# Loads in one order of need, attention outputs transposed by DMA, and matmul groups in halves, in a fused attention and gated-FFN kernel

## The chip, the cores and the metric

The kernel runs on one core of one Trainium2 chip. The metric is the device time of one execution in microseconds (us). "PE" is TensorE, "PEld" its weight loads, "DVE" VectorE, "ACT" ScalarE, "POOL" GpSimd, "SP" the sequencer that issues most DMAs. The time of a run is about 2 us more than the "span" of its profile, which goes from the first to the last instruction. "Clock" is the share of TensorE's full clock that was granted, as the profile recorded it. Up to the first record of a run (13.77 us in before) the views show 1.00, which says nothing: the matmuls there ran at half clock, as the distances between their starts show. "Segment" is one of the four stretches of 512 tokens.

## The reference

An attention with a compressive memory (4 segments of 512 tokens, 32 heads of 16) and a gated FFN read the same x; a gate per token mixes the two.

```python
x = A_x                                                  # 1 x 2048 x 512, bf16
g = sigmoid((x * gate_w).sum(-1, keepdims=True))
# attention, per segment s of 512 tokens:
logits = einsum('bhqd,bhkd->bhqk', qs, ks) * scale + mask    # causal inside the segment
a_dot  = einsum('bhqk,bhkd->bhqd', softmax(logits), vs)
a_mem  = (phi(qs) @ M) / (phi(qs) @ z + 1e-6)            # memory of the earlier segments
o      = gh * a_mem + (1 - gh) * a_dot                   # gh = sigmoid(beta), per head
M, z   = M + phi(ks)^T vs, z + sum phi(ks)
a = concat(o) @ wo
# FFN, F = 1792:
b = (relu(x @ W_gate) * (x @ W_up)) @ W_down
return g * a + (1 - g) * b
```

## The kernel before

All work is put into a list of tasks with an engine, a duration, a key and dependencies. A small planner in Python "runs" the list with these durations and so fixes the order of instructions on each engine; on the chip each engine works through its order and waits where an operand is late. Four PSUM banks (`wb`) serve every 512-column product, four more (`sp`) hold one tile of scores. The 32-row matmuls that write such a tile are called a "fill"; ACT then takes its exponentials ("exp"), and the matmuls of these with the values are called P·V.

The loads come from three queues. x arrives already transposed, by DMA:

```python
got_x[0] = load_xT(0)                                       # SP: DMA transpose of 512 x 512
got_q = [load_cols(nc.scalar, wq_sb, A_wq, 0, 256)]         # ACT queue
got_k = [load_cols(nc.scalar, wk_sb, A_wk, 0, 256)]
# ... second halves of wq and wk on ACT
got_v = load_cols(nc.sync, wv_sb, A_wv, 0, D)               # SP
got_g[0] = load_cols(nc.sync, wg_sb, B_W_gate, *FP[0])
got_u[0] = load_cols(nc.sync, wu_sb, B_W_up, *FP[0])
got_x[1] = load_xT(1)
for i in range(1, 4):                                       # POOL queue, at the same time
    got_g[i] = load_cols(nc.gpsimd, wg_sb, B_W_gate, *FP[i])
    got_u[i] = load_cols(nc.gpsimd, wu_sb, B_W_up, *FP[i])
# ... x of segments 2 and 3 on SP, wd and wo on POOL
```

A product over 512 of depth is one task of four matmuls; the down projection has tasks of 5, 5 and 4:

```python
def proj_mm(sl, w, c, seg):
    for ci in range(NC):                                    # NC = 4
        nc.tensor.matmul(bank(sl), lhsT=w[:, ci, c*P:(c+1)*P], rhs=xT[:, ci, seg*L:(seg+1)*L], ...)
a = plan.add("PE", 864, key, lambda: proj_mm(sl, wq_sb, c, seg), [got_x[seg], got_q[c // 2]] + war, ...)
```

The attention output of eight heads (128 channels) lies as tokens x channels and is needed as channels x tokens. PE transposes it against a diagonal matrix that also carries the token gate, and DVE evicts the result:

```python
def dg():                                                   # DVE, 4 per segment
    nc.vector.tensor_scalar(diag[seg % 2][:, t, :], ident[:], rcol[...], None, ALU.mult)
def tr():                                                   # PE, 4 matmuls, 16 times
    nc.tensor.matmul(bank(sl)[:, qb*P:(qb+1)*P], lhsT=o_sb[...], rhs=diag[i][:, qb, :], ...)
att["ot", seg, c] = plan.add("DVE", 690, key, lambda: nc.vector.tensor_copy(oT[i][:, c, :], bank(sl)), ...)
```

The softmax here doesn't subtract the row's maximum and nothing guards it: scores larger than these inputs give would overflow.

## Time and profile before

| | before |
|---|---|
| time, median of 3 runs | 313.22 us (312.8 to 313.27) |
| span of the profiled run | 311.0 us |
| PE busy | 290.3 us, 93% |
| mean granted clock | 0.983 |

Busy PE is a poor measure here, since matmuls are pipelined and their modelled ends overlap. What counts is the distance between starts. A 512-column matmul takes 0.216 us from start to start at full clock and 0.427 at half clock; four of them 0.86.

The page's 40 slices (7.8 us each) of the profile before, in tenths; "PEclk" is the granted clock, the last row the DMA rate:

```profile
PE   5646799999999999999999999999999999999995
...
PEclk9989599999999999999999999999999999999999
DMA  9999914100101001000010100000000000000000
GB/s 135 257 333 342 193 25 37 34 2 4 19 0 36 2 34 37 2 17 2 13 6 19 36 18 19 3 0 2 2 0 2 20 19 34 2 0 2 2 34 34
```

The first five slices are thin on PE and full on DMA; after that PE is full. The stretches of the profile before tell the same with the clock (columns: busy us and instructions of each engine, clock, DMA share, GB/s):

```profile
0.00:10.00 10.00, 4.02 (x9) 1.34 (x10) 0.72 (x7) 1.28 (x1) 6.10 (x12) 1.00 0.95 128
10.00:20.00 10.00, 5.44 (x16) 1.87 (x15) 3.52 (x7) 1.31 (x3) 6.29 (x10) 1.00 1.09 327
20.00:30.00 10.00, 8.21 (x48) 3.02 (x49) 6.26 (x17) 4.35 (x3) 1.85 (x2) 0.83 1.03 341
30.00:40.00 10.00, 6.69 (x34) 2.19 (x34) 2.78 (x9) 3.23 (x5) 1.23 (x2) 0.66 1.11 196
```

The timeline of PE before (start, length, line and operation, then in brackets the idle time ahead and what ended it) shows the three holes:

```profile
10.04 1.86 PE L321 MATMUL wb_125<-xT,wq_sb 128*128 128x512 bf16 x4 [4.16 <-DMA xT<-in_A_x_dram]
...
20.10 1.45 PE L391 MATMUL wb_125<-wv_sb,xT 128*128 128x512 bf16 x4 [4.62 <-DMA wv_sb<-in_A_wv_dram]
...
33.31 1.86 PE L321 MATMUL wb_124<-xT,wq_sb 128*128 128x512 bf16 x4 [5.00 <-DMA xT<-in_A_x_dram]
```

A group of four right after each hole took 1.4 to 1.9 us instead of 1.03, at half clock for all or part of it: at the first hole the clock had not yet risen (its first record is at 13.77 us), at the others it dropped at 20.60 and 30.84 us. Nine warming matmuls on zeros (1.86 to 5.9 us) did not help here, as PE stood idle after them until 10 us.

From 40 us on, PE hardly waits. Summing over starts, what PE spent beyond its unit costs (the usual distance to the next start: 0.216 us per 512-column matmul, 25 ns per P·V matmul, and so on) comes to 21.3 us after the first projection, 15 of them between 10 and 40 us and about 6 in the rest. The sum depends on how unit costs are rounded: with the medians of the traces as unit costs it is 19.7. One cost is there all the time, 80 times: a fill. The timeline of PE before:

```profile
59.79 1.02 PE L550 MATMUL wb_122<-xT,wu_sb 128*128 128x512 bf16 x4
60.75 0.39 PE L404 MATMUL sp<-QT_128,KTe_134 32*128 32x512 bf16 x4
```

The group starts at 59.79 and the fill at 60.75, 0.96 later instead of 0.86. The first weight load of the 32-row fill is recorded 4 ns before the fill starts, while those of full-array matmuls are recorded a whole matmul ahead. ACT spent 44.7 us waiting for fills, but ACT is only 62% busy and not the limit. The PE transposes appear as:

```profile
L501 PEld LDWEIGHTS <-o_sb 128*128 128x128 bf16 x48 | 3.6, 97 | 3.9 <-DVE o_sb L490 0.9 <-issue 0.9
L507 DVE CAST oT_162<-wb_125 128x512 bf16<-128x512 f32 x5 | 3.4, 682 | 0.8 <-PE wb_125 L501 0.8
```

These are groups (busy us, mean ns, idle us before); the evictions of all 16 outputs take 0.68 us each, and the 64 matmuls 4.7 us of PE from start to start.

### The profile page before, as it was taken

The numbers are of one execution on the slowest core, as the hardware profiler recorded it, in microseconds if no ns is written. First come the engines' busy times: TensorE is split into PE (matmuls) and PEld (weight loads), VectorE is DVE, ScalarE is ACT, GpSimd is POOL, SyncE is SP. The second block draws the span as 40 slices with busy tenths as digits, with TensorE's granted clock in tenths as the row PEclk, the third lists the DMA queues.
The fourth block names the chain that finished last, engine by engine and source line by source line (L and its number), as shares of the span: only waits on it lengthen the run. The fifth ranks groups of instructions, "written<-read, shape, count | busy, mean of one in ns | idle before, by whom it ended". The sixth has DMA issues, their size and how long they took to land.

```text
span 311.0 us, 6988 instructions
## 1 busy us (share of the span) xinstructions
PE 290.3 (93%) x2953; PEld 140.9 (45%) x2953; DVE 185.1 (60%) x458; ACT 192.7 (62%) x166; POOL 96.2 (31%) x150
## 2 busy tenths in 40 slices
PE   5646799999999999999999999999999999999995
PEld 1212245455445454545454545454545454545442
DVE  0236287957688153977884549594879271838211
ACT  1024388878787556877966657778796657792200
POOL 7342131524252323332333243333333333331000
PEclk9989599999999999999999999999999999999999
DMA  9999914100101001000010100000000000000000
GB/s 135 257 333 342 193 25 37 34 2 4 19 0 36 2 34 37 2 17 2 13 6 19 36 18 19 3 0 2 2 0 2 20 19 34 2 0 2 2 34 34
DMA packets 22302, 13.82 MB, mean 44 GB/s; under 512 B 15408, under 2 KB 21120, under 8 KB 22272
## 3 DMA queue, kind: packets, MB, share of 16 engines
q1 hardware_dynamic: 18736, 7.34, 11.6%
q0 software_dynamic: 1424, 4.99, 5.0%
q10 hardware_dynamic: 2112, 1.05, 2.0%
q8 instruction: 23, 0.38, 0.5%
q14 instruction: 7, 0.06, 0.1%
HBM read 7.61 MB, written 2.10 MB: 31 GB/s over the span
## 4 chain that ended last, share of the span: by engine, by line
PE 80%; DMA 8%; DVE 7%; SPq 2%; ACT 1%; issue 1%; DVEq 0%; ACTq 0%
PE wb_123 L550 9%; DMA xT<-in_A_x_dram 8%; PE wb_122 L573 8%; PE sp L404 8%; PE wb_125 L550 7%; PE wb_124 L550 6%; PE wb_122 L550 6%; PE wb_123 L573 6%; PE wb_124 L453 4%; PE wb_122 L453 3%; PE wb_122 L586 2%; PE wb_123 L321 2%; PE wb_122 L321 2%; PE wb_124 L321 2%; PE wb_123 L586 2%; SPq L177 2%
## 5 line engine op out<-in xcount | busy, mean ns | idle before, releaser
L550 PEld LDWEIGHTS <-wg_sb 128*128 128x128 bf16 x224 | 20.0, 97 | 23.4 <-issue 3.2
L550 PEld LDWEIGHTS <-wu_sb 128*128 128x128 bf16 x224 | 18.8, 98 | 23.1 <-issue 7.0
L425 ACT ACTIVATE E_154<-sp 128x2048 bf16<-128x2048 f32 x10 | 18.7, 1874 | 9.6 <-PE sp L404 8.3
L425 ACT ACTIVATE E_155<-sp 128x2048 bf16<-128x2048 f32 x10 | 18.8, 1876 | 7.7 <-PE sp L404 7.7
L425 ACT ACTIVATE E_158<-sp 128x2048 bf16<-128x2048 f32 x10 | 18.8, 1876 | 7.7 <-PE sp L404 5.0
L425 ACT ACTIVATE E_157<-sp 128x2048 bf16<-128x2048 f32 x10 | 18.8, 1881 | 7.2 <-PE sp L404 6.3
L425 ACT ACTIVATE E_159<-sp 128x2048 bf16<-128x2048 f32 x10 | 18.8, 1876 | 6.5 <-PE sp L404 5.2
L425 ACT ACTIVATE E_160<-sp 128x2048 bf16<-128x2048 f32 x10 | 18.8, 1876 | 4.5 <-PE sp L404 4.5
L425 ACT ACTIVATE E_161<-sp 128x2048 bf16<-128x2048 f32 x10 | 18.8, 1875 | 4.1 <-PE sp L404 3.7
L425 ACT ACTIVATE E_156<-sp 128x2048 bf16<-128x2048 f32 x10 | 18.8, 1876 | 4.1 <-PE sp L404 4.1
L550 PE MATMUL wb_123<-xT,wu_sb 128*128 128x512 bf16 x76 | 19.6, 381 | 0.0
L431 POOL TENSOR_SCALAR_AFFINE_SELECT E_154<-E_154 128x512 bf16<-128x512 bf16 x16 | 10.9, 696 | 26.3 <-ACT E_154 L425 26.3
L431 POOL TENSOR_SCALAR_AFFINE_SELECT E_156<-E_156 128x512 bf16<-128x512 bf16 x16 | 10.4, 663 | 27.8 <-ACT E_156 L425 27.8
L550 PE MATMUL wb_125<-xT,wg_sb 128*128 128x512 bf16 x72 | 18.5, 379 | 0.0
L431 POOL TENSOR_SCALAR_AFFINE_SELECT E_158<-E_158 128x512 bf16<-128x512 bf16 x16 | 10.7, 682 | 22.8 <-ACT E_158 L425 22.8
L431 POOL TENSOR_SCALAR_AFFINE_SELECT E_157<-E_157 128x512 bf16<-128x512 bf16 x16 | 10.5, 669 | 21.3 <-ACT E_157 L425 21.3
L431 POOL TENSOR_SCALAR_AFFINE_SELECT E_155<-E_155 128x512 bf16<-128x512 bf16 x16 | 10.5, 670 | 20.1 <-ACT E_155 L425 20.1
L431 POOL TENSOR_SCALAR_AFFINE_SELECT E_160<-E_160 128x512 bf16<-128x512 bf16 x16 | 10.4, 665 | 20.1 <-ACT E_160 L425 20.1
L550 PE MATMUL wb_123<-xT,wg_sb 128*128 128x512 bf16 x64 | 16.5, 380 | 0.1
L431 POOL TENSOR_SCALAR_AFFINE_SELECT E_161<-E_161 128x512 bf16<-128x512 bf16 x16 | 10.5, 670 | 19.7 <-ACT E_161 L425 19.7
L431 POOL TENSOR_SCALAR_AFFINE_SELECT E_159<-E_159 128x512 bf16<-128x512 bf16 x16 | 10.1, 646 | 20.6 <-ACT E_159 L425 20.6
L594 DVE TENSOR_SCALAR osb<-wb_122,ngcol 128x512 bf16<-128x512 f32 x8 | 6.0, 750 | 15.9 <-PE wb_122 L586 15.9
(585 smaller groups left out, 872.9 us busy)
## 6 DMA issues: line engine op xcount, KB each, us to landing
out_dram<-osb SPq DMA_DIRECT2D x16, 128.0 KB, 1.7
wd_sb<-in_B_W_down_dram POOLq DMA_DIRECT2D x2, 896.0 KB, 16.0
wg_sb<-in_B_W_gate_dram POOLq DMA_DIRECT2D x2, 384.0 KB, 13.8
wu_sb<-in_B_W_up_dram POOLq DMA_DIRECT2D x2, 384.0 KB, 14.6
wq_sb<-in_A_wq_dram ACTq DMA_DIRECT2D x2, 256.0 KB, 6.6
wk_sb<-in_A_wk_dram ACTq DMA_DIRECT2D x2, 256.0 KB, 10.7
wv_sb<-in_A_wv_dram SPq DMA_DIRECT2D x1, 512.0 KB, 17.8
wg_sb<-in_B_W_gate_dram POOLq DMA_DIRECT2D x1, 512.0 KB, 11.3
```

The source lines that it names most:

```text
L177: eng.dma_start(out=dst, in_=src)
L321: nc.tensor.matmul(bank(sl), lhsT=w[:, ci, c * P:(c + 1) * P], rhs=xT[:, ci, seg * L:(seg + 1) * L], start=(ci == 0), stop=(ci == NC - 1))
L404: nc.tensor.matmul(sp[:, j, off:off + n], lhsT=kt[32 * j:32 * j + 32, kb * P:(kb + 1) * P], rhs=QT[i][32 * j:32 * j + 32, kb * P:kb * P + ...
L425: b = plan.add("ACT", 1880, key, lambda Ef=Ef: nc.scalar.activation(Ef[:], sp[:], ACT.Exp, scale=SCALE), [a] + eread.get(n - RE, []), ACL)
L431: nc.gpsimd.affine_select(out=m, in_=m, compare_op=ALU.is_ge, fill=0.0, base=0, pattern=[[0, 4], [1, P]], channel_multiplier=-1)
L453: nc.tensor.matmul(bank(sl)[:, lo:lo + HW], lhsT=E[(5 * u + f) % RE][:, j, o:o + P], rhs=Vp[i][:, kb, 8 * c + h8, 0:HW], start=(q2 == 0 an ...
L550: nc.tensor.matmul(bank(sl), lhsT=w[:, ci, fv * P:(fv + 1) * P], rhs=xT[:, ci, seg * L:(seg + 1) * L], start=(ci == 0), stop=(ci == NC - 1))
L573: nc.tensor.matmul(bank(sl), lhsT=hT[(NF * seg + fv) % RH][:, lc:lc + P], rhs=wd_sb[:, fv, :], start=(fv == 0), stop=False)
L586: nc.tensor.matmul(bank(sl), lhsT=oT[i][:, ci, lc:lc + P], rhs=wo_sb[:, ci, :], start=False, stop=(ci == NC - 1))
L594: nc.vector.tensor_scalar(osb[0][:], bank(sl), ngcol[:, tt:tt + 1], None, ALU.mult)
```

## The change

Its intent: the first product should start early and nothing behind it should wait for a byte that is queued behind less urgent ones; PE and DVE should not spend time on transposing outputs; and a fill should not wait for a whole group. The core of the diff:

```diff
-    got_x[0] = load_xT(0)
-    got_q = [load_cols(nc.scalar, wq_sb, A_wq, 0, 256)]
-    ...
+    got_x0 = load(nc.sync, x0[:], x[0:L, :].rearrange("(t p) d -> p t d", p=P), L * D * 2)
+    got_q = [load_cols(nc.scalar, wq_sb, A_wq, 0, D)] * 2
+    got_k = [load_cols(nc.sync, wk_sb, A_wk, 0, D)] * 2
+    got_v = load_cols(nc.scalar, wv_sb, A_wv, 0, D)
+    load_gu(0)                       # all on SP from here, wg and wu pieces
+    load_gu(1)
+    got_x[1] = [load_xT(1)]
+    load_gu(2)
+    load_gu(3)
+    got_d = [load_wd(0, 7), load_wd(7, NF)]
+    got_o = load_cols(nc.sync, wo_sb, A_wo, 0, D)
+    got_x[2] = [load_xT(2)]
+    got_x[3] = [load_xT(3)]
...
+    def x0_tasks():                  # x of segment 0: 16 PE transposes, 4 evictions
+                    nc.tensor.transpose(tp[:, t*P:(t+1)*P], x0[:, t, c*P:(c+1)*P], ident[:])
...
+    def matmuls(key, deps, sl, ops, start=True, stop=True, prev=None):
+        for k in range(0, n, GM):    # GM = 2: halves; a continued group goes first
+            prev = plan.add("PE", 216 * ..., key - (CONT if k else 0), emit, deps, PEL, need=sl, after=prev)
...
-            a = plan.add("PE", 430, key, lambda pieces=pieces: qk(seg, c, pieces),
+            a = plan.add("PE", 430, key - QKP, lambda pieces=pieces: qk(seg, c, pieces),   # fills first
...
-        a = plan.add("PE", 230, key, tr, combs + [att["diag", seg]] + war, PEL, need=sl)
-        att["ot", seg, c] = plan.add("DVE", 690, key, lambda: nc.vector.tensor_copy(oT[i][:, c, :], bank(sl)), ...)
+        att["ot", u] = plan.add("SP", 1200, key, lambda: nc.sync.dma_start_transpose(
+            out=oT[i][:, c, :].rearrange("p (b q) -> p b q", b=4),
+            in_=osb2[:].rearrange("p q n -> p (q n)")), ...)
```

The token gate, which sat in `diag`, is now multiplied into the head gates (`grc`, 4 small DVE products per segment). The three parts are called "loads", "DMA transposes" and "halves" below. Loads include the arrival times that the planner assumes. Two small things changed that belong to no part: in the plan an up product no longer depends on its gate product, and the pieces of a down projection have one key and follow each other without a planned pause. "Before" thus differs from after with all three parts undone; the planner, run on a host without the chip, ends its plan for before at 293.0 us and for that kernel at 293.5.

More of the change, by code (lines that the diff above doesn't have):

```diff
@@ L31, with __init__ @@
 class Task:
-    def __init__(self, eng, dur, key, emit, deps=(), lat=100, need=None, frees=(), slot=None):
+    def __init__(self, eng, dur, key, emit, deps=(), lat=100, need=None, frees=(), after=None):
         self.eng, self.dur, self.key, self.emit = eng, dur, key, emit
         self.deps = [d for d in deps if d is not None]
-        self.lat, self.need, self.frees, self.slot = lat, need, tuple(frees), slot
-        self.done = None
-        self.start = None
+        self.lat, self.need, self.frees, self.after = lat, need, tuple(frees), after
+        self.avail = 0.0
 class Slot:
@@ L74, in run @@
         for t in self.tasks:
-            t.wait = len(t.deps)
+            t.wait = len(t.deps) + (t.after is not None)
             for d in t.deps:
                 users.setdefault(id(d), []).append(t)
+            if t.after is not None:
+                users.setdefault(id(t.after), []).append(t)
             for s in t.frees:
@@ L80, in run @@
         ready = [t for t in self.tasks if t.wait == 0]
-        for t in ready:
-            t.avail = 0.0
         busy = {}
@@ L112, in run @@
                         u.wait -= 1
-                        u.avail = max(getattr(u, "avail", 0.0), t.done)
+                        u.avail = max(u.avail, t.start + t.dur if u.after is t else t.done)
                         if u.wait == 0:
@@ L167 @@
     betab = sb([P, H], BF16, "betab")
-    clock = [3000.0]
+    E = [sb([P, 4, L], BF16, f"E{i}") for i in range(RE)]
+    x0 = E[RE - 1]
+    clock = [3500.0]
     plan = Plan(4)
     def arrival(nbytes):
-        clock[0] += nbytes / 380.0
+        clock[0] += nbytes / 340.0
         return plan.add("in%d" % len(plan.tasks), 0.0, 0.0, None, lat=clock[0])
@@ L187, in load_xT @@
                                     in_=x[seg * L:(seg + 1) * L, :])
-        return arrival(L * D * 2)
+        return arrival(L * D * 2 * 1.3)
     FP = [(0, 512), (512, 1024), (1024, 1408), (1408, F)]
     got_x, got_g, got_u = {}, {}, {}
-    got_x[0] = load_xT(0)
-    got_q = [load_cols(nc.scalar, wq_sb, A_wq, 0, 256)]
-    got_k = [load_cols(nc.scalar, wk_sb, A_wk, 0, 256)]
     nc.gpsimd.dma_start(out=betab[:], in_=A_beta.partition_broadcast(P))
@@ L197, with load_gu, load_wd @@
         nc.gpsimd.dma_start(out=gw[:], in_=gate_w.rearrange("(c p) -> p c", p=P))
-    got_q.append(load_cols(nc.scalar, wq_sb, A_wq, 256, 512))
-    got_k.append(load_cols(nc.scalar, wk_sb, A_wk, 256, 512))
-    got_v = load_cols(nc.sync, wv_sb, A_wv, 0, D)
-    got_gw = arrival(200000)
-    got_g[0] = load_cols(nc.sync, wg_sb, B_W_gate, *FP[0])
-    got_u[0] = load_cols(nc.sync, wu_sb, B_W_up, *FP[0])
-    got_x[1] = load_xT(1)
-    for i in range(1, 4):
-        got_g[i] = load_cols(nc.gpsimd, wg_sb, B_W_gate, *FP[i])
-        got_u[i] = load_cols(nc.gpsimd, wu_sb, B_W_up, *FP[i])
-    got_x[2] = load_xT(2)
-    got_x[3] = load_xT(3)
-    got_d = [load(nc.gpsimd, wd_sb[:, a:b, :],
-                  B_W_down.rearrange("(c p) n -> p c n", p=P)[:, a:b, :], (b - a) * P * D * 2)
-             for a, b in ((0, 7), (7, NF))]
-    got_o = load_cols(nc.gpsimd, wo_sb, A_wo, 0, D)
+    got_x0 = load(nc.sync, x0[:], x[0:L, :].rearrange("(t p) d -> p t d", p=P), L * D * 2)
+    got_q = [load_cols(nc.scalar, wq_sb, A_wq, 0, D)] * 2
+    got_k = [load_cols(nc.sync, wk_sb, A_wk, 0, D)] * 2
+    got_v = load_cols(nc.scalar, wv_sb, A_wv, 0, D)
+    got_gw = arrival(0)
+    def load_gu(i):
+        got_g[i] = load_cols(nc.sync, wg_sb, B_W_gate, *FP[i])
+        got_u[i] = load_cols(nc.sync, wu_sb, B_W_up, *FP[i])
+    def load_wd(a, b):
+        return load(nc.sync, wd_sb[:, a:b, :],
+                    B_W_down.rearrange("(c p) n -> p c n", p=P)[:, a:b, :], (b - a) * P * D * 2)
+    load_gu(0)
[7 more added lines that the diff above has]
+    got_x[3] = [load_xT(3)]
     ident = sb([P, P], BF16, "ident")
@@ L235 @@
     gb = sb([P, H], F32, "gb")
-    gcat = sb([P, NC, 2, 2, 8], F32, "gcat")
+    gcat = sb([P, NC, 2, 8], F32, "gcat")
+    grc = [sb([P, NC, 2, 4, 8], F32, f"grc{i}") for i in range(2)]
     def head_gates():
@@ L241, in head_gates @@
         gv, ev = (a.rearrange("p (c h) -> p c h", c=NC) for a in (gb, eb))
-        for b in range(2):
-            nc.vector.tensor_copy(gcat[:, :, 1, b, :], gv)
-            nc.vector.tensor_tensor(gcat[:, :, 0, b, :], ev, gv, ALU.mult)
+        nc.vector.tensor_copy(gcat[:, :, 1, :], gv)
+        nc.vector.tensor_tensor(gcat[:, :, 0, :], ev, gv, ALU.mult)
     got_eb = plan.add("ACT", 200, 0.0, lambda: nc.scalar.activation(
@@ L260 @@
     Vp = [sb([P, 4, H, 18], BF16, f"Vp{i}") for i in range(2)]
-    E = [sb([P, 4, L], BF16, f"E{i}") for i in range(RE)]
     oT = [sb([P, NC, L], BF16, f"oT{i}") for i in range(2)]
     hT = [sb([P, L], BF16, f"hT{i}") for i in range(RH)]
+    ob = [sb([P, 4, P], BF16, f"ob{i}") for i in range(2)]
     mbd = [sb([P, NC, 8, HW], BF16, f"mbd{i}") for i in range(2)]
@@ L271 @@
     ngcol = sb([P, NT], F32, "ngcol")
-    diag = [sb([P, 4, P], BF16, f"diag{i}") for i in range(2)]
     def bank(slot):
@@ L287, with emit, pe @@
     UNIT = 16000.0
+    def matmuls(key, deps, sl, ops, start=True, stop=True, prev=None):
+        n = len(ops)
+        for k in range(0, n, GM):
+            def emit(k=k):
+                for q in range(k, min(k + GM, n)):
+                    lhsT, rhs = ops[q]()
+                    nc.tensor.matmul(bank(sl), lhsT=lhsT, rhs=rhs, start=(start and q == 0),
+                                     stop=(stop and q == n - 1))
+            prev = plan.add("PE", 216 * (min(k + GM, n) - k), key - (CONT if k else 0), emit, deps,
+                            PEL, need=sl, after=prev)
+            deps = ()
+        return prev
+    def x0_tasks():
+        done = []
+        for c in range(NC):
+            sl = Slot(1)
+            def pe(c=c, sl=sl):
+                tp = wb[sl.banks[0]][:].bitcast(BF16)
+                for t in range(4):
+                    nc.tensor.transpose(tp[:, t * P:(t + 1) * P], x0[:, t, c * P:(c + 1) * P],
+                                        ident[:])
+            a = plan.add("PE", 240, K(-9), pe, [got_x0], PEL, need=sl)
+            cp = nc.scalar.copy if c % 2 else nc.vector.tensor_copy
+            done.append(plan.add(
+                "ACT" if c % 2 else "DVE", 430, K(-9), lambda c=c, sl=sl, cp=cp: cp(
+                    xT[:, c, 0:L], wb[sl.banks[0]][:].bitcast(BF16)[:, 0:L]),
+                [a], DVL, frees=[sl]))
+        return done
     def gate_tasks(seg):
@@ L300, in pe @@
                                      stop=(t == 3 and ci == NC - 1))
-        a = plan.add("PE", 420, key, pe, [got_x[seg], got_gw], PEL, need=sl)
+        a = plan.add("PE", 420, key, pe, got_x[seg] + [got_gw], PEL, need=sl)
         b = plan.add("DVE", 170, key, lambda: nc.vector.tensor_scalar(
@@ L310, in gate_tasks, with gt, proj_mm @@
         att["ng", seg] = plan.add("DVE", 340, key, ng, [c], DVL)
-        def dg():
+        def gt():
             for t in range(4):
-                nc.vector.tensor_scalar(diag[seg % 2][:, t, :], ident[:],
+                nc.vector.tensor_scalar(grc[seg % 2][:, :, :, t, :], gcat[:],
                                         rcol[:, 4 * seg + t:4 * seg + t + 1], None, ALU.mult)
-        att["diag", seg] = plan.add("DVE", 1000, key, dg, [c] + [
-            att.get(("tr", seg - 2, k)) for k in range(NC)], DVL)
-    def proj_mm(sl, w, c, seg):
-        for ci in range(NC):
-            nc.tensor.matmul(bank(sl), lhsT=w[:, ci, c * P:(c + 1) * P],
-                             rhs=xT[:, ci, seg * L:(seg + 1) * L],
-                             start=(ci == 0), stop=(ci == NC - 1))
+        war = [att.get(("comb", 4 * seg - 5, p)) for p in range(2)]
+        att["gate", seg] = plan.add("DVE", 800, key, gt, [c, got_gates] + war, DVL)
+    def proj_mm(w, c, seg):
+        return [lambda ci=ci: (w[:, ci, c * P:(c + 1) * P], xT[:, ci, seg * L:(seg + 1) * L])
+                for ci in range(NC)]
     def proj_q(seg, c):
@@ L329, in proj_q @@
         war = [att.get(("pv", u - RQ, p)) for p in range(2)]
-        a = plan.add("PE", 864, key, lambda: proj_mm(sl, wq_sb, c, seg),
-                     [got_x[seg], got_q[c // 2]] + war, PEL, need=sl)
+        a = matmuls(key, got_x[seg] + [got_q[c // 2]] + war, sl, proj_mm(wq_sb, c, seg))
         prj["q", seg, c] = plan.add("DVE", 690, key, lambda: nc.vector.tensor_copy(
@@ L351, in proj_k @@
         war = [att.get(("pv", u - RQ, p)) for p in range(2)]
-        a = plan.add("PE", 864, key, lambda: proj_mm(sl, wk_sb, c, seg),
-                     [got_x[seg], got_k[c // 2]] + war, PEL, need=sl)
+        a = matmuls(key, got_x[seg] + [got_k[c // 2]] + war, sl, proj_mm(wk_sb, c, seg))
         kt, e = [], []
@@ L387, in proj_v @@
         war = [att.get(("pv", 4 * seg - 8 + c, 1)) for c in range(NC)] + [att.get(("mz", seg - 2))]
-        def pe():
-            for ci in range(NC):
-                nc.tensor.matmul(bank(sl), lhsT=xT[:, ci, seg * L + t * P:seg * L + (t + 1) * P],
-                                 rhs=wv_sb[:, ci, :], start=(ci == 0), stop=(ci == NC - 1))
-        a = plan.add("PE", 864, key, pe, [got_x[seg], got_v] + war, PEL, need=sl)
+        t0 = seg * L + t * P
+        a = matmuls(key, got_x[seg] + [got_v] + war, sl, [
+            lambda ci=ci: (xT[:, ci, t0:t0 + P], wv_sb[:, ci, :]) for ci in range(NC)])
         prj["v", seg, t] = plan.add("DVE", 690, key, lambda: nc.vector.tensor_copy(
@@ L433, in attention @@
             masks.append(plan.add("POOL", 640 * len(diags), key, mk, [b], POL))
-        combs = []
-        o_sb = {}
+        osb2 = ob[u % 2]
         for p in range(2):
@@ L481, in comb @@
                 cf = rpool.tile([P, m, 2, 8], F32, name=f"cf{m}")
-                nc.vector.tensor_tensor(cf[:], rs[:], gcat[:, c, 0:m], ALU.mult)
-                tb = rpool.tile([P, m, 2, 8, DH], BF16, name=f"tb{m}")
+                nc.vector.tensor_tensor(cf[:], rs[:], grc[i][:, c, 0:m, 2 * p:2 * p + 2, :],
+                                        ALU.mult)
+                dst = osb2[:, 2 * p:2 * p + 2].rearrange("p q (h e) -> p q h e", e=DH)
+                tb = None
+                if seg:
+                    tb = rpool.tile([P, m, 2, 8, DH], BF16, name="tb")
                 for k in range(m):
-                    nc.vector.tensor_tensor(tb[:, k], v[k][:, :, :, 0:DH],
+                    nc.vector.tensor_tensor(tb[:, k] if seg else dst, v[k][:, :, :, 0:DH],
                                             cf[:, k, :, :, None].to_broadcast([P, 2, 8, DH]),
@@ L488, in comb @@
                 if seg:
-                    o = rpool.tile([P, 2, 8, DH], BF16, name="o_sb")
-                    nc.vector.tensor_tensor(o[:], tb[:, 0], tb[:, 1], ALU.add)
-                    o_sb[p] = o
-                else:
-                    o_sb[p] = tb[:, 0]
-            combs.append(plan.add("DVE", 1950 if seg else 950, key, comb, [a, got_gates], DVL,
-                                  frees=[sl]))
-        key = KA(u - LEAD, 14000)
-        sl = Slot(1)
-        def tr():
-            for qb in range(4):
-                nc.tensor.matmul(bank(sl)[:, qb * P:(qb + 1) * P],
-                                 lhsT=o_sb[qb // 2][:, qb % 2].rearrange("p h e -> p (h e)"),
-                                 rhs=diag[i][:, qb, :], start=(qb == 0), stop=(qb == 3))
+                    nc.vector.tensor_tensor(dst, tb[:, 0], tb[:, 1], ALU.add)
+            att["comb", u, p] = plan.add(
+                "DVE", 1950 if seg else 950, key, comb,
+                [a, att["gate", seg], att.get(("ot", u - 2))], DVL, frees=[sl])
+        key = KA(u - LEAD, 14000)
         war = [ffn.get(("o", seg - 2, q)) for q in range(4)]
-        a = plan.add("PE", 230, key, tr, combs + [att["diag", seg]] + war, PEL, need=sl)
-        att["tr", seg, c] = a
-        att["ot", seg, c] = plan.add("DVE", 690, key, lambda: nc.vector.tensor_copy(
-            oT[i][:, c, :], bank(sl)), [a], DVL, frees=[sl])
+        att["ot", u] = plan.add("SP", 1200, key, lambda: nc.sync.dma_start_transpose(
+            out=oT[i][:, c, :].rearrange("p (b q) -> p b q", b=4),
+            in_=osb2[:].rearrange("p q n -> p (q n)")),
+            [att["comb", u, p] for p in range(2)] + war, 2500)
     def memory(seg):
@@ L546, in ffn_tasks @@
             piece = next(k for k, (a, b) in enumerate(FP) if a <= fv * P < b)
-            def mm(w, sl, fv=fv):
-                for ci in range(NC):
-                    nc.tensor.matmul(bank(sl), lhsT=w[:, ci, fv * P:(fv + 1) * P],
-                                     rhs=xT[:, ci, seg * L:(seg + 1) * L],
-                                     start=(ci == 0), stop=(ci == NC - 1))
-            g = plan.add("PE", 864, key, lambda mm=mm, sl=gsl: mm(wg_sb, sl),
-                         [got_x[seg], got_g[piece]], PEL, need=gsl)
+            g = matmuls(key, got_x[seg] + [got_g[piece]], gsl, proj_mm(wg_sb, fv, seg))
             rg = []
@@ L560, in ffn_tasks @@
             r = plan.add("ACT", 600, key - RL, relu, [g], ACL, frees=[gsl])
-            u = plan.add("PE", 864, key + 1, lambda mm=mm, sl=usl: mm(wu_sb, sl),
-                         [got_x[seg], got_u[piece], g], PEL, need=usl)
+            u = matmuls(key + 1, got_x[seg] + [got_u[piece]], usl, proj_mm(wu_sb, fv, seg))
             hs.append(plan.add("DVE", 690, key - RL, lambda sl=usl, rg=rg, fv=fv: (
@@ L569, in ffn_tasks @@
             lc, tt = qb * P, 4 * seg + qb
-            def down(f0, f1, sl=sl, lc=lc):
-                for fv in range(f0, f1):
-                    nc.tensor.matmul(bank(sl), lhsT=hT[(NF * seg + fv) % RH][:, lc:lc + P], rhs=wd_sb[:, fv, :],
-                                     start=(fv == 0), stop=False)
             prev = None
-            for k, (f0, f1) in enumerate(((0, 5), (5, 10), (10, 14))):
-                prev = plan.add("PE", 216 * (f1 - f0), key + k, lambda d=down, a=f0, b=f1: d(a, b),
-                                hs[f0:f1] + got_d + [prev]
-                                + [att["ot", seg, c] for c in range(NC)], PEL,
-                                need=sl)
+            for f0, f1 in ((0, 5), (5, 10), (10, 14)):
+                prev = matmuls(key, hs[f0:f1] + got_d
+                               + [att["ot", 4 * seg + c] for c in range(NC)], sl, [
+                    lambda fv=fv, lc=lc: (hT[(NF * seg + fv) % RH][:, lc:lc + P], wd_sb[:, fv, :])
+                    for fv in range(f0, f1)], start=(f0 == 0), stop=False, prev=prev)
                 for fv in range(f0, f1):
                     hread.setdefault(NF * seg + fv, []).append(prev)
-            def o(sl=sl, lc=lc):
-                for ci in range(NC):
-                    nc.tensor.matmul(bank(sl), lhsT=oT[i][:, ci, lc:lc + P], rhs=wo_sb[:, ci, :],
-                                     start=False, stop=(ci == NC - 1))
-            a = plan.add("PE", 864, key + 4, o, [prev, got_o], PEL, need=sl)
+            a = matmuls(key, [got_o], sl, [
+                lambda ci=ci, lc=lc: (oT[i][:, ci, lc:lc + P], wo_sb[:, ci, :]) for ci in range(NC)],
+                start=False, prev=prev)
             ffn["o", seg, qb] = a
@@ L599 @@
     LEAD, FLAG, RL = 2.0, 0.0, 40000.0
+    GM, CONT, QKP = 2, 10000.0, 1e6
+    got_x[0] = x0_tasks()
     for seg in range(NSEG):
```

## The prediction

> **What bounds the kernel now.** The span is 311.0 us, of which TensorE (PE) is the limit in two different ways. From about 40 us on it is packed: stretches of the timeline show PE busy 20.0 of 20 us nearly everywhere, and start-to-start spacing of the 512-column matmuls is 217 ns with no slack (927 or so of them are 200 us). Filling the score tile costs about 0.41 us each of 80 times: 0.30 streaming and 0.107 us more for the matmul before it. P·V is 1280 x 25 ns = 32 us. Before 40 us PE is starved: by its instruction starts I count only about 14.5 us of useful work in the first 40 us, so 25 us are lost. The waits and the chain name the causes: x transposed by DMA lands at 10.0 us (wait 4.2), wv at 20.06 (wait 4.6), x of segment 1 at 33.3 (wait 5.0, "DMA xT" 8% of the chain). The granted clock is half in part of 20-24 us and in 31-38 us, after those holes. The tail from last matmul to end is about 3.5 us.
>
> **What changes.**
> 1. Loads: one order of need; x of segment 0 comes as rows, 16 PE transposes plus four evictions. From the landings I estimate x and wq at 6.8 us, first projection at about 9 us (little earlier than now, 10.04), but wk, wv by 9.6, the first gate/up pieces by 13, x of segment 1 by about 21 us, when PE needs it at about 23. The 16 transposes cost 1 to 2 us at a cold clock. The Trainium skill, "TensorE: Matmul & The Clock Gate" (Part 4), says transposes do not raise the clock; so I count about 2 us of cold projections. "DMA: Bandwidth & Descriptors" (Latency and other measured facts) gives DMA transposes 261 GB/s; this trace disagrees: 84 to 110 GB/s moved in 6-10 us, while the first one was in flight. So x of segment 1 will hold the queues about 4 us, not the 2 planned. Gain of this part: 12 to 16 us.
> 2. Attention outputs by DMA: 64 matmuls against diag go, 16 x 0.28 = 4.5 us of PE, all on the critical path after 40 us; also 16 DVE copies of 0.68 us (11 us) and 64 diag products of 0.246 us, off the path. 16 DMA transposes of about 2.5 us to landing come in, hidden. Gain: 4 to 5 us.
> 3. Halves with score fills between: the exp of a fill starts sooner (ACT waited some 45 us for scores), but ACT is not the limit, each fill still costs its 0.107 us, and PE after 40 us has only about 1 us of stalls. Gain: about 0, at worst a loss of 2 if PE reaches fills before ACT is done.
>
> **Sum.** 9.0 start + 2.0 cold + 273.7 PE work without diag + 3.6 tail + about 5 stalls (most before 25 us, where DVE must evict about 11 us of projections for 10 us of PE) = 293.5 us span; the timed run is about 2.2 us longer: **296 us**, range 290 to 303. Faster by over 2%: 0.95; within 2%: 0.04; slower: 0.01.
>
> **Right or wrong.** Right: PE near 10 tenths from about 12 us on, no wait over 2 us for wv or x of segment 1, no half clock after 15 us, no diag group, time from 40 us to the end shorter mainly because more work was done before 40 us. The score fill entry stays near 0.107 us.
>
> **What would make it wrong.** The DMA transpose of x holding back the gate/up pieces; PE stalled at fills by ACT; output transposes queued behind the loads; PSUM banks held longer by half groups.

## The result, and the profile after

| | before | after |
|---|---|---|
| time, median of 4 runs each | 313.25 us | 292.15 us (292.1 to 292.2) |
| ratio, 95% interval | | 0.9327 (0.9311 to 0.9343) |
| span of the profiled run | 311.0 us | 290.4 us |
| first projection starts | 10.04 us | 7.79 us |
| PE time beyond unit costs, after that start | 21.3 us | 7.0 us |
| last matmul to the end | 3.5 us | 3.55 us |
| mean clock | 0.983 | 1.000 |

A ratio here is the mean time of one kernel's fast runs over the mean of the other's in the same rounds, so it is not quite the ratio of the medians. The 20.6 us of span split into 2.25 (earlier start), 14.3 (less waiting) and 4.7 (64 matmuls gone); that is 21.3, 0.7 more than measured, since unit costs are rounded.

The slices of the profile after, same rows as before:

```profile
PE   7899999999999999999999999999999999999995
...
PEclk9999999999999999999999999999999999999999
DMA  6999962010110201100103010000100110010011
GB/s 178 341 277 344 187 121 43 2 21 18 29 29 21 56 18 20 20 18 2 36 2 76 20 36 3 19 2 2 20 18 3 36 38 27 12 20 0 0 36 36
```

The stretches after:

```profile
0.00:10.00 10.00, 7.80 (x33) 3.60 (x33) 2.26 (x10) 2.46 (x3) 5.11 (x13) 1.00 0.77 219
10.00:20.00 10.00, 9.27 (x60) 4.02 (x60) 7.84 (x19) 5.55 (x6) 1.26 (x2) 1.00 1.10 295
20.00:30.00 10.00, 10.00 (x89) 4.36 (x89) 9.20 (x25) 9.03 (x11) 4.15 (x7) 1.00 1.09 346
30.00:40.00 10.00, 10.00 (x111) 4.83 (x110) 9.03 (x20) 8.50 (x8) 3.40 (x5) 1.00 1.07 154
```

PE ran 293 matmuls in the first 40 us, against 107 before. The timeline of PE after has one short hole after the transposes, and a fill that sits, with two groups for v, between the two halves of a group (11.49 and 14.35, bank 130):

```profile
6.10 0.61 PE L315 MATMUL wb_133<-ident,E_83 128*128 128x128 bf16 x4 [0.22 <-DMA E_83<-in_A_x_dram]
...
7.79 1.26 PE L300 MATMUL wb_133<-xT,wq_sb 128*128 128x512 bf16 x4
...
10.62 1.04 PE L300 MATMUL wb_131<-xT,wk_sb 128*128 128x512 bf16 x4 [0.71 <-DMA wk_sb<-in_A_wk_dram]
11.49 0.59 PE L300 MATMUL wb_130<-xT,wk_sb 128*128 128x512 bf16 x2
...
14.02 0.39 PE L434 MATMUL sp<-QT_134,KTe_140 32*128 32x512 bf16 x4
14.35 0.60 PE L300 MATMUL wb_130<-xT,wk_sb 128*128 128x512 bf16 x2
...
20.34 1.04 PE L300 MATMUL wb_133<-xT,wq_sb 128*128 128x512 bf16 x4
```

The line at 20.34 is the first projection of segment 1, with no wait: its x had landed at 18.7. The output transposes are now DMA issues; the line of the profile after's DMA view gives the median us from issue to landing:

```profile
oT_162<-ob_182 SPq DMA_TRANSPOSE x4, 2.8
```

### The profile page after: what moved, and what is told of

Its sections match the earlier page's. It is cut to its first block, busy times and chain, and to the rows that moved or that the text cites. A ratio compares the mean times of both kernels' runs of the same rounds, so it can differ in the third digit from the quotient of the medians.

```text
span 290.4 us, 6923 instructions
## 1 busy us (share of the span) xinstructions
PE 282.2 (97%) x2905; PEld 138.5 (48%) x2905; DVE 176.5 (61%) x442; ACT 194.6 (67%) x168; POOL 88.5 (30%) x141
## 4 chain that ended last, share of the span: by engine, by line
PE 90%; ACT 3%; DMA 3%; DVE 1%; issue 0%; POOL 0%; SPq 0%; ACTq 0%
PE wb_131 L300 24%; PE wb_130 L300 21%; PE wb_133 L300 13%; PE wb_132 L300 10%; PE sp L434 9%; PE wb_132 L482 7%; DMA wk_sb<-in_A_wk_dram 3%; PE wb_130 L482 2%; PE wb_133 L482 1%; PE wb_133 L473 1%; ACT E_79 L455 1%; ACT E_78 L455 1%; ACT E_77 L455 1%; ACT E_76 L455 1%; PE wb_132 L542 1%; PE wb_133 L542 1%
## 5 line engine op out<-in xcount | busy, mean ns | idle before, releaser
L300 PEld LDWEIGHTS <-wu_sb 128*128 128x128 bf16 x224 | 20.2, 98 | 26.3 <-issue 4.9
L300 PE MATMUL wb_130<-xT,wg_sb 128*128 128x512 bf16 x88 | 23.2, 380 | 0.0
L300 PE MATMUL wb_133<-xT,wu_sb 128*128 128x512 bf16 x72 | 18.9, 380 | 0.0
L300 PE MATMUL wb_131<-xT,wu_sb 128*128 128x512 bf16 x72 | 18.7, 380 | 0.0
L461 POOL TENSOR_SCALAR_AFFINE_SELECT E_79<-E_79 128x512 bf16<-128x512 bf16 x16 | 10.2, 651 | 20.1 <-ACT E_79 L455 20.1
L461 POOL TENSOR_SCALAR_AFFINE_SELECT E_77<-E_77 128x512 bf16<-128x512 bf16 x16 | 10.3, 662 | 18.7 <-ACT E_77 L455 18.7
L576 ACT ACTIVATE rg<-wb_130 128x512 bf16<-128x512 f32 x22 | 13.1, 594 | 3.5 <-PE wb_130 L300 3.4
```

The source lines that it names most:

```text
L300: nc.tensor.matmul(bank(sl), lhsT=lhsT, rhs=rhs, start=(start and q == 0), stop=(stop and q == n - 1))
L461: nc.gpsimd.affine_select(out=m, in_=m, compare_op=ALU.is_ge, fill=0.0, base=0, pattern=[[0, 4], [1, P]], channel_multiplier=-1)
L576: nc.scalar.activation(rg[0][:], bank(sl), ACT.Relu)
```

## The experiments

Medians are of four runs in the fast state unless said otherwise. "Before" ran beside each batch and had medians of 313.07, 312.78 and 312.88 us in the three batches. Kernels of one batch shared a chip. In my variants the profile does not number the tiles of a name. Their profiles often miss some 5% of the matmul records; idle times put down to "issue" in them are mostly such holes.

### 1. Undo one part, and do one part alone

Six kernels make, with before and after, all eight combinations of the three parts (but for the two small things named above, which are in all of them and not in before).

Halves undone in after, `undo_halves`:

```diff
-    GM, CONT, QKP = 2, 10000.0, 1e6
+    GM, CONT, QKP = 5, 0.0, 0.0
```

> After, but with whole matmul groups (4 or 5 at a time), no priority for continuing a group and none for score fills. Theory A (PE is packed after 40 us, so only starting earlier and doing less PE work pays): 291.5 to 293.5 us, the same as after, with the same 0.107 us ahead of each fill. Rival B (the chain score fill, exp, score fill bounds the kernel, and halves shorten it): slower by 5 us or more, 297 us and up.

DMA transposes undone in after, `undo_dma_tr`: the code of before for `diag`, `tr` and the eviction, in place of `grc` and

```diff
-        att["ot", u] = plan.add("SP", 1200, key, lambda: nc.sync.dma_start_transpose(...
+        a = plan.add("PE", 230, key, tr, combs + [att["diag", seg]] + war, PEL, need=sl)
+        att["ot", u] = plan.add("DVE", 690, key, lambda: nc.vector.tensor_copy(oT[i][:, c, :], bank(sl)), ...)
```

> After, but the attention outputs are again transposed by PE against diag, with the evictions and diag products on DVE. Theory A: the 64 matmuls cost 4.7 us of PE by the trace of before, all on the path, so 296 to 298 us. Rival B (PE work of that size disappears in waits on the exp chain): under 294 us. Rival C (DVE, 14 us lighter without the evictions, is what was freed): over 300 us.

Loads undone in after, `undo_loads`: the load block of before (with its planned arrival times) and

```diff
-    got_x[0] = x0_tasks()
```

> After, but with the loads of before (x of segment 0 by DMA transpose, three queues). Theory A: first projection again at about 10 us, waits of 4 to 5 us for wv and x of segment 1 and a half clock after each, so 292.2 + 16.6 (2.25 later start, 14.35 more stalls before 40 us) = 308 to 310 us. Rival B: most of the gain is in the halves, so under 302 us.

Loads alone, `only_loads` (the first two undone together):

> Before, with the new loads alone (halves and DMA transposes of the outputs undone in after). Theory A: 313.2 - 16.6 = 296 to 298 us. Rival B: above 303 us.

In a second batch, halves alone (`only_halves`) and DMA transposes alone (`only_dma_tr`), made in the same way:

> Before, with halves and the priority of score fills alone. With the new loads and PE transposes the halves cost 2.0 us (298.69 against 296.71), with DMA transposes they save 2.4. Theory A2 (halves spread few-tenths stalls differently in each schedule, no fixed worth): within 3 us of before, either sign, 310 to 316. Rival D (halves are bad wherever the attention outputs need PE and a PSUM bank): slower by 2 us or more, 315 and up.

> Before, with the DMA transposes of the outputs alone. PE loses 4.7 us of matmuls. In the new loads without halves that moved the time by 2.2 us only (296.71 to 294.52), with halves by 6.5. Theory A2: 3 to 5 us gained here, 308.5 to 310.5. Rival E (worth nothing by itself without halves): over 311.5.

| loads | DMA transposes | halves | kernel | median us | ratio to before (95%) |
|---|---|---|---|---|---|
| | | | before | 313.07 / 312.78 | 1 |
| | | x | only_halves | 314.37 | 1.0045 (1.0007 to 1.0084) |
| | x | | only_dma_tr | 311.29 | 0.9956 (0.9931 to 0.9981) |
| | x | x | undo_loads | 308.13 | 0.9843 (0.9818 to 0.9868) |
| x | | | only_loads | 296.71 | 0.9493 (0.9459 to 0.9528) |
| x | | x | undo_dma_tr | 298.69 | 0.9545 (0.9522 to 0.9568) |
| x | x | | undo_halves | 294.52 | 0.9411 (0.9391 to 0.943) |
| x | x | x | after | 292.15 | 0.9327 (0.9311 to 0.9343) |

What follows:

- **Loads are worth 16 us in every company.** From pairs of ratios times 313: 15.9 alone, 17.1 with DMA transposes, 15.7 with halves, 16.2 with both. Theory A's 16.6 is met within 1 us by all four, and rival B (halves first) has fallen.
- **DMA transposes are worth 1.4 to 2.6 us without halves and 6.3 to 6.8 with them.** Theory A expected 4.7 whatever the company. All its figures for this part missed: `undo_dma_tr` came to 298.7 where 296 to 298 stood, `only_dma_tr` to 311.3 where 308.5 to 310.5 stood. Rivals C (over 300 us, DVE the thing freed) and E (over 311.5, worth nothing without halves) are not met either, E by 0.2 us only.
- **Halves cost 1.4 to 1.6 us beside PE transposes and save 2.6 to 3.5 us beside DMA transposes.** `undo_halves` at 294.5 lies above theory A's range and below rival B's. A2 and D cannot be told apart by `only_halves`, as 314.4 fits A2's range and misses D's 315 by less than the spread of runs.

So two of the parts are not additive, by about 4.6 us, and this is the same under old and new loads (4.9 and 4.3 us by the ratios); it is no noise. One half of it can be seen. The waits of PE in `undo_halves` and in `only_dma_tr` (us in total, times, longest) have, near their heads:

```profile
PE sp L434 <- ACT E L455: 2.2, 2, 1.1
```

```profile
PE sp L430 <- ACT E L451: 2.2, 2, 1.1
```

In after the same waits are three of 0.2 us, and in `only_loads` one of 0.2. The timeline of PE in `undo_halves` shows the first:

```profile
111.96 1.04 PE L300 MATMUL wb<-xT,wg_sb 128*128 128x512 bf16 x3
114.09 0.40 PE L434 MATMUL sp<-QT,KTe 32*128 32x384 bf16 x8 [1.09 <-ACT E L455]
```

After one group PE has nothing next in its order but the fill, and the fill's PSUM tile is still being read by an exp that ends at 114.04. That occurs twice, 2.2 us in all, near 113 and 190 us. DMA transposes without halves thus give back 2.2 of their 4.7 us as these two waits; the order that the halves bring avoids them. The other half, why halves beside PE transposes cost 1.5 to 2 us, has no single wait behind it: without the warming matmuls' own and those put down to "issue", the waits of `undo_dma_tr` are 3.1 us and those of `only_loads` 2.7, in items of 0.2 to 1.3 us.

The planner shows where most of the interaction comes from. Run on a host with its own durations, it ends its plan at these times (us; the two rows assume different arrival times and are not to be compared with each other):

| planned end | neither | halves | DMA transposes | both |
|---|---|---|---|---|
| loads of before | 293.0 (before) | 295.7 | 292.1 | 289.4 |
| new loads | 295.9 | 297.5 | 294.2 | 291.5 |

By the plan halves cost 1.5 us beside PE transposes and save 2.7 beside DMA transposes under the new loads, 4.3 apart, as measured; under the old loads the two differ by 5.5, against 4.9 measured. So the interaction is already in the order that the planner makes: PE's planned idle time is 7.5 us in `only_loads`, 9.1 in `undo_dma_tr`, 9.5 in `undo_halves` and 6.8 in after. Only why such a planner makes a worse order in one case than in another stays open.

The idea that halves work by shortening the chain of exps is refuted by the same runs. The exps in after and in `undo_halves` (the view of the exp's line; first and last start):

```profile
L455 ACT ACTIVATE E_83<-sp x10: 1871/1877/1877, 35.9 to 247.4; 128x2048 bf16<-128x2048 f32 x10
```

```profile
L455 ACT ACTIVATE E<-sp x80: 1872/1877/1912, 14.9 to 259.0; 128x2048 bf16<-128x2048 f32 x80
```

The last exp starts 11.6 us earlier with halves, and the kernel ends 2.4 us earlier. Beside PE transposes the two even part: the last exp starts 9.8 us earlier in `undo_dma_tr` (251.8) than in `only_loads` (261.6), and the kernel ends 2.0 us later. After the exps comes FFN work that PE would have had to do anyway.

### 2. Single matmuls instead of halves

`singles`: after, with

```diff
-    GM, CONT, QKP = 2, 10000.0, 1e6
+    GM, CONT, QKP = 1, 10000.0, 1e6
```

> After, with groups cut into single matmuls in place of halves, so that a score fill waits for one matmul at most. Theory J (shorter waits for fills are what halves buy): 290.5 to 292. Theory A2 (a cut only reshuffles tenths of stalls): between 290.5 and 295 with no sign to be told beforehand, and the exp chain not shorter than 235 us.

Measured: 295.83 us (295.65 to 295.89), ratio 0.9455 (0.9429 to 0.9482), so 3.7 us slower than after, though a fill waits for less. Theory J has fallen; the time lies even 0.8 us above A2's range. PE's time beyond unit costs, after the first projection, rose from 7.0 to 10.2 us. Among its waits, those for DVE's combination of the attention outputs, which holds PSUM banks, are 1.6 us in all, and after has none of them over 0.2:

```profile
PE wb L473 <- DVE tb L518: 0.9, 2, 0.5
PE wb L300 <- DVE tb L518: 0.7, 2, 0.4
```

A finer cut is thus no better by itself. What a cut is worth depends on the whole order that the planner makes from it, and the plan itself ends at 296.7 us here, 5.2 later than that of after.

### 3. Which part of the loads

`x0_by_dma`: after, with

```diff
-    got_x0 = load(nc.sync, x0[:], x[0:L, :].rearrange("(t p) d -> p t d", p=P), L * D * 2)
+    got_x[0] = [load_xT(0)]
...
-    got_x[0] = x0_tasks()
```

> After, with x of segment 0 brought by one DMA transpose at the head of the same ordered queue, in place of plain rows and 16 PE transposes. Theory A (the order of need is what pays, the PE transposes only buy the earlier start): the transpose lands at 8 to 10 us and holds back wk and wv by some 3 us, so first projection at about 9.5 us against 7.8, and 294 to 296 us. Rival B (the PE transposes are the heart of the gain: the DMA transpose starves everything behind it): over 299 us.

Measured: 296.74 us (295.23 to 296.95), ratio 0.9478 (0.9447 to 0.9509), 4.6 us slower than after. Theory A was right in kind and its range 0.7 us short. Its timeline of PE:

```profile
9.69 3.57 PE L300 MATMUL wb<-xT,wq_sb 128*128 128x512 bf16 x8 [3.99 <-DMA xT<-in_A_x_dram]
13.06 3.16 PE L300 MATMUL wb<-xT,wk_sb 128*128 128x512 bf16 x8
```

It starts 1.9 us later, and eight matmuls take 3.4 us from start to start instead of 1.7: PE had idled and the clock was half from 8.8 to 15.6 us. The forgotten term was the clock: 14 matmuls at half clock took 2.9 us more than at full.

`weights_pool`: after, with the gate and up pieces 1 to 3, wd and wo issued from POOL:

```diff
     def load_gu(i):
-        got_g[i] = load_cols(nc.sync, wg_sb, B_W_gate, *FP[i])
+        eng = nc.gpsimd if i else nc.sync
+        got_g[i] = load_cols(eng, wg_sb, B_W_gate, *FP[i])
```

> After, with the gate and up pieces 1 to 3, wd and wo issued from the POOL queue as before, so that they run beside the urgent loads instead of behind them; nothing else changed. Theory A: queues share the bandwidth, so wv lands near 17 us instead of 11.4 and x of segment 1 near 28 us instead of 18.7; PE waits 4 to 8 us more and the time is 296 to 300 us. Rival B (the number of queues is indifferent, as the bytes are the same and PE has other work): within 1 us of after, 291.5 to 293.2.

Measured: 306.0 us (305.51 to 306.94), ratio 0.9788 (0.976 to 0.9815), far outside both. But the experiment had a flaw, which the first line of PE's waits shows:

```profile
PE wb L316 <- POOL ident L224: 7.7, 1, 7.7
```

POOL makes the identity for the PE transposes, and in this kernel it first issued its loads, until 12.6 us. So POOL was mended to make the identity first, `weights_pool_ident_first`:

```diff
+    ident = sb([P, P], BF16, "ident")          # moved ahead of the loads, with its
+    nc.gpsimd.memset(ident[:], 0.0)            # memset and affine_select
     load_gu(0)
```

> The mended form of the run with weights on the POOL queue: there PE stood 7.7 us waiting for the identity, because POOL was issuing loads; here POOL makes the identity before it issues them. Theory A (one queue keeps the urgent bytes first): transposes again start near 6 us, wk and wv land near 13 and 15 us and x of segment 1 at 32 us, so waits of 2 to 3, 1 to 2 and 3 to 5 us come back: 298 to 303 us. Rival F (what cost 14 us was only the identity): 291.5 to 294.

Measured: 306.33 us (305.74 to 306.78), ratio 0.9791 (0.9762 to 0.9819), again 14 us slower than after and 3 us beyond theory A's range; rival F has fallen. Its timeline of PE:

```profile
11.90 2.33 PE L301 MATMUL wb<-xT,wk_sb 128*128 128x512 bf16 x6 [2.81 <-DMA wk_sb<-in_A_wk_dram]
27.30 1.89 PE L301 MATMUL wb<-xT,wu_sb 128*128 128x512 bf16 x4 [5.02 <-DMA wu_sb<-in_B_W_up_dram]
31.69 1.89 PE L301 MATMUL wb<-xT,wq_sb 128*128 128x512 bf16 x4 [1.96 <-ACT E L456]
```

The first up piece, which landed at 14.0 us in after, now landed at 27.25, and x of segment 1 at 31.64 instead of 18.69. (The third wait is put down to an exp; x of segment 1 landed 0.05 us before its end.) The bytes are the same, and the weights on the other queue came early for nothing. The waits are 9.8 us; the clock, at half from 12.4 to 15.8 and from 26.0 to 36.3 us, made most of the rest. The Trainium skill, "DMA: Bandwidth & Descriptors" (section "Issuing engines are not separate DMA queues"), says that DMAs of all issuing engines run on the same 16 engines and interleave; this run agrees, and puts a price on it: the transfers that are needed last take bandwidth from those needed first.

So the order in one queue carries about 14 of the 16 us, and the PE transposes of x carry 4.6. The sum is not 16, so the two overlap; that each spares some of the same waiting is likely and not shown. The planned order is the same in after and here. Whether a plan with truer arrival times would have lost less with the three queues was not tried.

### 4. The warming matmuls

`no_junk`: after, with

```diff
-    for k in range(9):
+    for k in range(0):
```

> After, without the nine warming matmuls on zeros. The recorded clock of after is full from 7.87 us, just as the 16 PE transposes end. Theory G (the transposes are enough to raise the clock): within 0.6 us of after, full clock by 8 us. Rival H (the skill's page: transposes do not count as PE work for the clock): the first projections run at half clock until 11.3 us or later, 1.5 to 2.5 us slower than after, 293.7 to 294.7 us.

Measured: 292.62 us (292.45 to 292.88), ratio 0.9355 (0.9324 to 0.9385), 0.5 us slower than after. The time is theory G's, but the first projections ran at half clock, as rival H had it. The timeline of PE:

```profile
5.96 1.89 PE L315 MATMUL wb<-ident,E 128*128 128x128 bf16 x16 [5.96 <-POOL bd L235]
7.64 3.61 PE L300 MATMUL wb<-xT,wq_sb 128*128 128x512 bf16 x8
11.05 0.85 PE L300 MATMUL wb<-xT,wk_sb 128*128 128x512 bf16 x3
```

The eight query matmuls ran at half clock (0.427 us each), until full clock was recorded at 11.1 us. They lost about 1.7 us, but wk landed only at 10.8 us, and PE would have waited for it anyway: after waited until 10.62. So only 0.4 us reached the end.

The run does not decide whether transposes count for the clock, since there were too few. In each trace the recorded changes of clock lie 3.41 us or a multiple of it apart (in before 13.77, 20.60, 24.01, 30.84 and 37.66 us). Take the stretches of 3.41 us between such instants in the first 42 us of 13 profiles, those at half clock: it rose at the end of each that PE's matmuls, counted from start to start, filled to 83% or more, and of none that they filled to 76% or less (nothing lay between). In `no_junk` the transposes filled one stretch to 51%. The profile after does decide (stretches as above, ending at its first record):

```profile
1.04:4.45 3.41, 2.59 (x7) 0.94 (x8) 0.62 (x6) 1.28 (x1) 2.99 (x6) 1.00 0.54 174
4.45:7.87 3.42, 3.20 (x21) 2.02 (x20) 0.69 (x2) 0.59 (x1) 1.92 (x4) 1.00 1.04 256
```

2.6 us of warming matmuls in the first stretch did not raise the clock; 1.2 us of them with 1.7 us of transposes in the second did. It is the same in `undo_halves`, `undo_dma_tr` and `singles` (2.3 to 2.5 us of warming matmuls did not; 1.3 to 1.6 with 1.6 to 1.7 of transposes did). So the transposes counted (in the built program these 16 matmuls carry the flag of transpose mode). They also ran at full clock where it was granted before them, as in `only_loads` (first record 5.18 us), 56 ns from start to start:

```profile
6.08 1.07 PE L315 MATMUL wb<-ident,E 128*128 128x128 bf16 x16 [0.48 <-DMA E<-in_A_x_dram]
```

The Trainium skill, "TensorE: Matmul & The Clock Gate" (Part 4, PE-mode transpose), says that the full clock does not engage for transposes and that they do not count as busy in the same way; these runs contradict both.

### 5. An attempt at a faster version

`seq_loads`: after, with each of x of segment 0, wq, wk and wv split in halves that SP and ACT bring together, and six warming matmuls:

```diff
-    got_x0 = load(nc.sync, x0[:], ...)
-    got_q = [load_cols(nc.scalar, wq_sb, A_wq, 0, D)] * 2
+    def both(t, ap):
+        return [load_rows(nc.sync, t, ap, 0, 2), load_rows(nc.scalar, t, ap, 2, 4)]
+    got_x0 = both(x0, x[0:L, :])
+    got_q = [both(wq_sb, A_wq)] * 2            # wk and wv alike
```

> After, with x of segment 0, wq, wk and wv each split in two halves that the two hardware queues bring at the same time, so that one of the four arrives before the next starts, and with six warming matmuls in place of nine. By the landings of after: x at 4.6 us in place of 6.06, first projection at about 6.4 in place of 7.8, wk at 8 in place of 10.57 so its 0.7 us wait goes. Theory A: 2 us gained, 289.5 to 291 us. Rival I (DVE, which must evict the projections, sets the pace to 20 us): within 0.7 us of after.

Measured: five fast runs of 290.93 to 292.12 us and one, the profiled one, slow at 350 us and clock 0.757; ratio of the fast runs 0.9313 (0.9287 to 0.9339). The interval covers that of after (0.9327), and the two did not run side by side, so a gain of 0.5 us is possible and not shown; the 2 us of theory A are refuted. The profile of the slow run is used for landings alone, before any long matmul work: x landed at 4.6 us, 1.5 earlier than in after, but wq at 7.8 us, 1.3 later than in after, so the first projection began at 7.5 instead of 7.79. Serving x first put wq behind it. Why the two, the same 1 MB, were complete 1.3 us later than in after is not shown.

## Why the prediction was right or wrong

The time (296 predicted, 292.15 measured) and the main reason were right. Term by term of the predicted sum:

| term | predicted us | measured us |
|---|---|---|
| start of the first projection | 9.0 | 7.79 |
| cold projections | 2.0 | about 0.2 |
| PE work without diag | 273.7 | 272.1 (286.85 - 7.79 - 7.0) |
| tail | 3.6 | 3.55 |
| stalls | about 5 | 7.0, the 0.2 included |
| timed run beyond span | 2.2 | 1.75 |

- **Loads, "12 to 16 us": right**, at the upper end or 1 us above it: 15.7 to 17.1 in the four comparisons.
- **"about 2 us of cold projections": wrong.** In after the clock was full from 7.87 us and the matmuls of the queries took 0.215 us from start to start. The step that failed is the one taken from the skill, that transposes do not raise the clock; it also forgot the warming matmuls that ran until 5.7 us. The two together raised it (experiment 4). With the warming matmuls removed, eight matmuls were indeed cold. At half clock, 16 transposes took 1.7 us, as "1 to 2 us" had it.
- **"x of segment 1 will hold the queues about 4 us": wrong.** It landed 1.8 us after the load ahead of it, and in 16 to 20 us the DMA engines moved 217 to 222 GB/s, against 336 to 347 in the 4 us before. The 84 to 110 GB/s that I had taken from before were of three queues in the first 10 us. The 261 GB/s that the prediction took from the Trainium skill's "DMA: Bandwidth & Descriptors" (Latency and other measured facts) was nearer.
- **DMA transposes of outputs, "4 to 5 us": right only as a mean.** The PE time was sized well (4.7 us), but "all on the critical path" failed: alone they gave 1.4 us, in after 6.8. That 4 to 5 lies between is luck, and so is the fit of the sum with halves: 4 to 5 was predicted for both together and 5.2 measured (after against `only_loads`).
- **Halves, "about 0, at worst a loss of 2": wrong by company.** In after they save 2.6 us, beside PE transposes they lose 1.4 to 1.6. The reason given, that each fill keeps its entry cost, was right: the matmul ahead of a fill took 96 ns longer in the median, before and after (the prediction's 107 is a mean with a few waits in it).
- **"most before 25 us, where DVE must evict": wrong place.** Of the 7.0 us beyond unit costs, 1.6 lie before 20 us, and the largest of these is the wait for wk, not for DVE. Some 4 to 5 us, by the unit costs taken, are spread after 40 us, in pieces of a few tenths.

Of the signs that were to tell right from wrong, all that concerned loads came true: no hole over 2 us for wv or x of segment 1, no half clock, no diag group.

## What to carry to other kernels

Ask of every early load which product waits for it, and put the loads into one queue in that order; a second queue that brings later weights at the same time takes their bandwidth, and each PE hole is paid twice, by the wait and by the half clock after it. Price a removed piece of work on the packed engine as an upper bound only: where a planner fixes the order, taking work away can open a wait that gives half of it back, so test the parts in combination before crediting any, first in the planner, whose own planned end showed the interaction here without a run. And before splitting work more finely so that one chain runs earlier, check that this chain ends the kernel: here it ended 11.6 us earlier for 2.4 us of gain.

## What the Trainium skill lacked or had wrong

- Wrong here: "TensorE: Matmul & The Clock Gate" (Part 4, PE-mode transpose) says that the full clock does not engage for transposes, which do not count as busy in the same way. Sixteen of them ran 56 ns apart at full clock, and 1.7 us of them with 1.2 us of warming matmuls raised the clock where 2.6 us of warming matmuls did not. The page gives the time of a single transpose (275 to 390 ns) and lacks the distance in a row: 107 ns at half clock, 56 at full.
- The same page (Part 3) says that weight loads overlap with running matmuls only where row groups differ. Here full-array matmuls, each with a weight load of 97 ns of its own, started 216 ns apart, so their loads overlapped in the same row groups. No page gives a price for the switch to 32-row matmuls: the matmul ahead of a fill took 96 ns longer (median), a P·V matmul 78 ns, 80 times in the kernel.
- "DMA: Bandwidth & Descriptors" gives 261 GB/s for DMA transposes with a non-contiguous middle dimension and 350 to 400 for the contiguous case ("Latency and other measured facts"). In a stream on one queue I read 217 to 222 GB/s over two stretches of 2 us that also held plain loads; beside two other queues, early in the kernel, 84 to 110. It has no time for a small SBUF-to-SBUF transpose: 128x512 bf16 took 2.4 us from issue to landing.
- The same page says that issuing from several engines at once only saves issue time. It lacks the loss: with late weights on a second queue the first up piece landed at 27.25 us instead of 14.0, and the kernel took 14 us more.
- None of the pages I read says that loads issued from POOL hold up POOL's own work: issuing took 0.75 us each, and with waits the identity was made at 12.9 us instead of 3.1.
